# A gated recurrence with an MLP behind it: MLP products on 64 by 128 of the array in place of 64 by 64

## The chip, the core and the metric

The kernel runs on one core of one Trainium2 chip. The metric is device time in microseconds (us) of one execution. The core has five engines with queues of their own: TensorE (PE in the profile; its weight loads are listed apart as PEld), VectorE (DVE), ScalarE (ACT), GpSimd (POOL) and SyncE (SP, which here issues the DMAs). TensorE writes only to PSUM, and the other engines empty it. Each engine works through its instructions in the order in which they were issued, so that order is part of the kernel.

## The reference

An attention-like recurrence over 768 steps, for 4 batches and 8 heads of 40 channels, and behind it an MLP with a gelu. All values are float32, the MLP's weights float64 on arrival.

```python
for t in range(S):
    y[:, :, t] = einsum('bhd,bhde->bhe', rt, state)
    Sa = einsum('bhde,bhe->bhd', state, at)
    state = state * wt[:, :, None, :] - einsum('bhd,bhe->bhde', Sa, bt) \
            + einsum('bhd,bhe->bhde', vt, kt)
...
x = y.transpose(0, 2, 1, 3).reshape(B * S, H * D)      # 3072 x 320
h = x @ w_in                                           # w_in 320 x 2048
g = h * (1.0 / (1.0 + exp(-1.702 * h)))
out = g @ w_out                                        # w_out 2048 x 320
```

## The kernel before

**Units.** The sequence is cut into 12 chunks of 64 steps. A unit is one chunk of two batches with all heads; unit `i` is chunk `c = i // 2`, pair of batches `p = i % 2`, so there are 24 units. Within a chunk the recurrence is solved as matrix products: decays (`ps_cum`), scores (`ps_A`, `ps_RV`, `ps_N`), a triangular inverse in five levels (`ps_level`, then `ps_Q`, `ps_T21`), the known part (`ps_B`), the solution (`ps_X`) and the outputs with the new state (`ps_y`). From chunk to chunk goes only the state, `zraw`, so unit `i` waits for the state of unit `i - 2`, and the two units of a chunk are independent.

**The array in quarters.** Every matmul uses a quarter of TensorE's 128x128 array: 64 rows of contraction (a half of the partitions, `HALF`) by 64 columns of weights. `QUARTERS` lists the four (row half, column half) pairs, and four matmuls that follow each other go to the four quarters. One float32 matmul of the program is two MATMUL and two LDWEIGHTS instructions in the profile.

**The state's turn** (L891 to L905, in `solve`). From the second chunk on, `zr` gets the state times the decay `wz` (L891). `state_turned` then multiplies it by an identity, 16 matmuls of 64x40 weights and 40 moving columns, into `ps_zT`; two copies (L904) put it into `zT`, from which `read_state` (L907) computes `ps_rz`.

**The MLP** (`mlp`, L1021 to L1070), once for a chunk, 256 rows of x. `up(q, m, k)` is a task of 4 matmuls: quarters of 64x64 of `w_in_sb`, 256 moving columns of x. `q` counts 4 groups of the hidden width, `m` two halves of a group and `k` five steps of contraction, so a chunk has 40 up tasks. Ten of them fill one PSUM pair (two banks), and one gelu of 128x1024 (L1034) empties it to `g`. `down(p)` has 8 tasks of 8 matmuls, with 64 columns of `g` as weights and 320 moving columns of `w_out_sb`; two instructions empty `ps_down` into `ob` (L1058, L1060), and a DMA stores it.

**The order.** The kernel is first written as a list of tasks (`plan.add`), each with the engines that may take it, the time that it is thought to take there, what it reads, writes and waits for, a rank, and the PSUM pair that it holds (there are 4 pairs). `Plan.order` (L103) is a planner that runs through time: whenever an engine is free it takes the task of lowest rank that is ready. It charges TensorE for instruction fetch as well, in blocks of 256 instructions. `paced` (L223) releases MLP tasks, which have the highest ranks and so fill gaps, evenly over time; `moved` (L242) applies a table of small shifts of rank, engine and release (`FOUND`, L260). The tasks are then issued in the planned order (L1098).

**Weights.** The float64 weights come in 8 pieces and are turned into float32 by ScalarE, VectorE and GpSimd (`weight`, L466 on; `rebased` to `joined`). No up task can run before its first pieces and the first chunk's x are there.

Of the kernel before, what the change touches and what calls it, by code (L numbers as in the profile page):

```python
# [49 lines left out]
class Task:  # L50
    def __init__(self, rank, engines, fn, pair, most, size):
        self.instr, self.sbuf, self.table = engines.pop("instr", -Plan.EVENTS) + Plan.EVENTS, engines.pop("sbuf", False), engines.pop("table", None)
        self.rank, self.fn, self.pair, self.most, self.size = rank, fn, pair, most, size
        self.engines = self.may = engines
        self.after, self.then, self.release = set(), [], 0.0
        self.load = False


class Plan:

    BLOCK, FETCH, AHEAD = 256, 3460.0, 300.0
    FIRST, EVENTS = 63, 0.24
    BESIDE, LARGE, BESIDE_LARGE = 0.35, 327700, 0.5
    COLD, WINDOW, SHARE = 2.0, 2600.0, 0.45
    SWITCH = 1290.0
    DELAY = {"PE": 300.0, "DVE": 60.0, "ACT": 60.0, "POOL": 150.0, "SP": 800.0}  # L70

    BEGIN = {"PE": 0.0, "ACT": 3300.0, "DVE": 6500.0, "POOL": 10000.0, "SP": 800.0}
    LATENCY, RATE, SPREAD = 2010.0, 417.0, 1.3
# [29 lines left out]
    def order(self):  # L103
        for n, t in enumerate(self.tasks):
            t.n, t.left, t.ready, t.then = n, len(t.after), 0.0, []
        for t in self.tasks:
            for o in t.after:
                o.then.append(t)
        free = dict(self.BEGIN)
        pairs = [0.0] * self.pairs  # L110
        held, users = {}, {k: len(v) for k, v in self.of_pair.items()}
        coming = [(t.release, t.n) for t in self.tasks if not t.left]
        heapq.heapify(coming)
        able, now, wire, out, many = [], 0.0, 0.0, [], set()
        running, last, worked = [], {}, []
        table = "exp"

        def fits(t, margin=0.0):
            if t.pair is None or t.pair in held:
                return True  # L120
            clear = sum(p <= now - margin for p in pairs)
            if t.most is None:

                return clear > len({o.pair[0] for o in able if o.most is not None and o.pair not in held and not any(k[0] == o.pair[0] for k in many)})
            return clear > 0 and sum(k[0] == t.pair[0] for k in many) < t.most

        issued, begun, shared = self.FIRST, 0.0, 0.0

        def fetch(at):
            took = self.FETCH  # L130
            for _ in range(3):
                took = self.FETCH + sum(w * max(0.0, min(y, at + took) - max(x, at)) for x, y, w in running[-10:])
            return took

        def unread(t, e):

            return max((x + 60.0 for o, x in last.get(t.pair, {}).items() if o != e), default=0.0) if t.pair is not None and e != "PE" else 0.0

        def takes(t, start):

            busy = sum(max(0.0, y - max(x, start - self.WINDOW)) for x, y in worked[-60:])
            return t.engines["PE"] * (self.COLD if busy < self.SHARE * self.WINDOW else 1.0)

        def fetched(t, start):

            ns = takes(t, start) / t.instr
            at, left, block = start, t.instr, begun
            room = self.BLOCK - issued % self.BLOCK
            while left >= room:
                at += room * ns  # L150
                left -= room
                at = block = max(at, block + fetch(block))
                room = self.BLOCK
            return at + left * ns, block

        def ahead(t):

            return (issued % self.BLOCK + t.instr) * fetch(begun) / self.BLOCK - (now + takes(t, now) - begun)

        while coming or able:  # L160
            while coming and coming[0][0] <= now:
                able.append(self.tasks[heapq.heappop(coming)[1]])
            able.sort(key=lambda t: (t.rank, t.n))
            took = None
            for e in free:
                if free[e] <= now:
                    took = None
                    took = next((t for t in able if e in t.may and fits(t) and unread(t, e) <= now), None)
                    if took and e == "PE" and ahead(took) > self.AHEAD:

                        took = next((t for t in able if e in t.may and fits(t) and ahead(t) < min(self.AHEAD, ahead(took))), took)
                    if took:
                        break
            if not took:
                later = [x for x in (*free.values(), *pairs, *(unread(t, e) for t in able for e in t.may)) if now < x < float("inf")]
                later += [coming[0][0]] if coming else []
                if not later:
                    return out
                now = min(later)
                continue  # L180
            t = took
            able.remove(t)
            t.engine = e
            end = now + t.engines[e]
            if e == "ACT" and t.table:
                t.load, table = t.table != table, t.table
                end += self.SWITCH if t.load else 0.0
            if e == "PE":
                end, begun = fetched(t, now)
                worked.append((now, min(end, now + takes(t, now))))  # L190
                issued += t.instr
            if e == "POOL" or e == "DVE" and t.sbuf:

                shared = max(now, shared) + t.engines[e]
                end = max(end, shared)
            free[e] = end
            if e == "SP":
                wire = max(wire, end + self.LATENCY)
                running.append((wire, wire + self.SPREAD * t.size / self.RATE, self.BESIDE_LARGE if t.size > self.LARGE else self.BESIDE))
                end = wire = running[-1][1]  # L200
            if t.pair is not None:
                if e != "PE":
                    last.setdefault(t.pair, {})[e] = end
                if t.pair not in held:
                    held[t.pair] = next(i for i, p in enumerate(pairs) if p <= now)
                    pairs[held[t.pair]] = float("inf")
                    if t.most is not None:
                        many.add(t.pair)
                t.bank = held[t.pair]
                users[t.pair] -= 1  # L210
                if not users[t.pair]:
                    many.discard(t.pair)
                    pairs[t.bank] = end + self.DELAY[e]
            for o in t.then:
                o.ready = max(o.ready, end + (0.0 if o.engines.keys() == {e} else self.DELAY[e]))
                o.left -= 1
                if not o.left:
                    heapq.heappush(coming, (max(o.ready, o.release), o.n))
            t.start = now
            out.append(t)  # L220
        return out

    def paced(self, groups, rounds, window, share):  # L223


        best = None
        for n in range(rounds):
            out = self.order()
            end = max(t.start + t.engines[t.engine] for t in out)
            if best is None or end < best[0]:  # L230
                best = end, [(t, {**vars(t)}) for t in out]
            for g, then in zip(groups, groups[1:]):
                whole, done, begin = sum(t.engines["PE"] for t in g), 0.0, g[0].ready
                for t in g:
                    new = begin + share * (then[0].ready - begin) * done / whole - window
                    t.release = new if n == 0 else 0.5 * (t.release + new)
                    done += t.engines["PE"]
        for t, kept in best[1]:
            vars(t).update(kept)
        return [t for t, _ in best[1]]  # L240

    def moved(self, moves):  # L242

        groups = {}
        for t in self.tasks:
            key = (t.fn.__code__.co_firstlineno, t.rank, tuple(sorted(t.engines)), t.pair)
            groups.setdefault(key, []).append(t)
# [44 lines left out]
def rwkv7_gelu_quick(ctx: ExitStack, tc: tile.TileContext, time_d, v_d, w_d, wc_d, ak_d, b_d, rv_d, w_in, w_out, out):  # L292
# [60 lines left out]
    def dve(n):  # L353
        return {"DVE": 170.0 + 1.03 * n}
# [205 lines left out]
    def slot(b, u, f):  # L560
        return 4 * u + 2 * b + f
# [619 lines left out]
```

## Time and profile before

| | |
|---|---|
| time, median of 2 runs | 688.07 us (687.27 to 688.87) |
| span of the profiled execution | 685.1 us, 42187 instructions |
| mean granted TensorE clock | 0.989 of full speed |
| TensorE matmuls in the span | 19488 instructions, as many weight loads |
| of these `ps_up` / `ps_down` | 3840, busy 252.4 us / 3072, busy 240.5 us |
| gelu `g<-ps_up` 128x1024 | 48, mean 1026 ns |
| `zr<-zraw,wz` on VectorE, 128x320 | 22, median 518 ns |
| `kh<-time,G` on GpSimd, 128x320 | 19, mean 887 ns |
| chain of waits, share of the span | PE 90%, of it `ps_down` 30% and `ps_up` 29%; issue 2% |
| DMA | 69.73 MB, mean 102 GB/s |
| DMA queue of the instructions | 153 packets, 2.51 MB |

How to read it: the busy time of an engine is the time in which at least one of its instructions runs. For TensorE that is not its pace: a matmul lasts much longer than the time after which the next one may start, so four or more overlap. The pace is read from stretches in which one kind of matmul runs alone: length over count. "Issue" in the chain is time for which the profile shows no cause. A wait is charged to what ended last.

### The profile page before, as it was taken

To read this page: it belongs to the slowest core of one execution; us is meant where nothing else is said; L and a number is where in the kernel's file an instruction comes from. 1 tells how busy PE (TensorE), PEld (TensorE's weight loads), DVE (VectorE), ACT (ScalarE), POOL (GpSimd) and SP (SyncE) were. 2 spreads that over 40 slices of the span, in tenths; PEclk is the share of its full clock that TensorE was granted. 3 is DMA by queue.
4 is the path that set the end of the run, shared out by engine and by line. 5 is a ranking of instruction groups with operands and counts; after the bars stand their busy time and mean duration, and the time that the engine had idled before them with its cause. 6 is when DMAs were issued, how large, how long until landed. Compare 5 with 4: busy or idle time off the path is not lost.

```text
span 685.1 us, 42187 instructions
## 1 busy us (share of the span) xinstructions
PE 649.1 (95%) x19488; PEld 563.2 (82%) x19488; DVE 459.0 (67%) x916; ACT 323.5 (47%) x670; POOL 184.5 (27%) x215
## 2 busy tenths in 40 slices
PE   3657999999999999999999999999999999999997
PEld 3556888997899899988888897788788799899895
DVE  6686989767867767857785677867666766675001
ACT  4566633454555664564455445355354454262110
POOL 5354546324123212323213130322411421300000
PEclk9989999999999999999999999999999999999999
DMA  7993434414414413432404413413411411200100
GB/s 238 314 318 118 163 119 129 122 33 127 124 42 116 144 34 107 133 90 85 132 21 125 137 40 111 145 37 115 138 40 55 136 52 43 70 14 17 56 12 20
DMA packets 35312, 69.73 MB, mean 102 GB/s; under 512 B 5440, under 2 KB 14656, under 8 KB 35136
## 3 DMA queue, kind: packets, MB, share of 16 engines
q1 hardware_dynamic: 35136, 67.03, 32.6%
q8 instruction: 153, 2.51, 1.5%
q14 instruction: 23, 0.19, 0.1%
HBM read 59.15 MB, written 7.86 MB: 98 GB/s over the span
## 4 chain that ended last, share of the span: by engine, by line
PE 90%; DVE 3%; DMA 2%; issue 2%; ACT 1%; POOL 0%; SPq 0%; ACTq 0%; DVEq 0%
PE ps_down L343 30%; PE ps_up L343 29%; PE ps_level L343 9%; PE ps_y L343 5%; PE ps_B L343 5%; PE ps_X L343 3%; PE ps_A L343 2%; PE ps_N L343 2%; PE ps_RV L343 2%; PE ps_rz L343 1%; PE ps_zT L343 1%; PE ps_cum L343 1%; PE ps_T L343 1%; DMA rv<-in_rv 1%; DMA extra<-in_w_out 1%
## 5 line engine op out<-in xcount | busy, mean ns | idle before, releaser
L343 PE MATMUL ps_up<-xT_all,w_sb 64*64 64x256 f32 x3840 | 252.4, 377 | 1.0 <-issue 0.8
L343 PE MATMUL ps_down<-w_sb,g 64*64 64x320 f32 x3072 | 240.5, 430 | 0.5 <-issue 0.3
L343 PEld LDWEIGHTS ps_up<-xT_all,w_sb 64*64 64x64 f32 x3840 | 171.7, 133 | 15.9 <-issue 1.9
L343 PEld LDWEIGHTS ps_down<-w_sb,g 64*64 64x64 f32 x3072 | 136.1, 133 | 36.3 <-issue 1.1
L755 POOL TENSOR_TENSOR EX<-ES,quads 128x512 f32<-128x512 f32 x31 | 41.7, 1345 | 117.7 <-DVE ES L748 76.5
L1034 ACT ACTIVATE g<-ps_up 128x1024 f32<-128x1024 f32 x48 | 49.2, 1026 | 49.0 <-PE ps_up L343 48.6
L797 ACT COPY W<-ps_level 128x512 f32<-128x512 f32 x56 | 32.8, 586 | 69.3 <-PE ps_level L343 67.6
L343 PEld LDWEIGHTS ps_level<-W,EX 64*64 64x64 f32 x2560 | 59.4, 134 | 5.7 <-ACT EX L753 0.2
L799 DVE TENSOR_TENSOR E<-two,ps_level 128x256 f32<-128x256 f32 x80 | 33.1, 415 | 35.7 <-ACT W L797 32.0
L343 PE MATMUL ps_level<-W,EX 64*64 64x64 f32 (+1 forms) x2560 | 56.4, 217 | 0.0
L753 ACT ACTIVATE EX<-ES,quads 128x256 f32<-128x256 f32 x80 | 36.3, 501 | 32.5 <-DVE ES L748 31.9
L665 POOL TENSOR_TENSOR ak<-ak,FT 128x512 f32<-128x512 f32 x16 | 20.6, 1288 | 76.4 <-DMA ak<-in_ak 62.3
L343 PE MATMUL ps_level<-PT,EX 64*64 64x64 f32 (+2 forms) x1280 | 33.1, 236 | 8.3 <-DVE EX L769 4.5
L343 PEld LDWEIGHTS ps_level<-PT,EX 64*64 64x64 f32 x1280 | 30.9, 139 | 11.8 <-issue 6.5
L937 ACT COPY B<-ps_B 128x416 f32<-128x416 f32 (+1 forms) x35 | 17.2, 491 | 47.2 <-PE ps_B L343 47.0
L748 DVE STREAM_TRANSPOSE ES<-E 128x256 f32<-128x256 f32 x80 | 35.2, 442 | 4.4
L343 PE MATMUL ps_y<-M,bh 64*64 64x104 f32 (+1 forms) x768 | 35.1, 247 | 0.1
L343 PE MATMUL ps_y<-RV,kh 64*64 64x104 f32 (+1 forms) x768 | 35.1, 247 | 0.0
L999 POOL TENSOR_TENSOR x<-zr,FT 128x128 f32<-128x128 f32 x48 | 25.0, 552 | 29.7 <-DVE zr L989 14.2
L673 POOL TENSOR_TENSOR kh<-time,G 128x320 f32<-128x320 f32 x19 | 16.8, 887 | 52.4 <-PE ps_y L343 39.2
L343 PE MATMUL ps_B<-RV,A 64*64 64x104 f32 (+1 forms) x768 | 29.3, 252 | 1.4 <-issue 1.4
L343 PEld LDWEIGHTS ps_B<-RV,A 64*64 64x64 f32 x768 | 25.9, 137 | 5.4 <-issue 1.6
(136 smaller groups left out, 1111.0 us busy)
## 6 DMA issues: line engine op xcount, KB each, us to landing
time<-in_time SPq DMA_DIRECT2D x24, 320.0 KB
ak<-in_ak SPq DMA_DIRECT2D x48, 160.0 KB
rv<-in_rv SPq DMA_DIRECT2D x48, 160.0 KB
xT_all<-x_dram SPq DMA_DIRECT2D x48, 160.0 KB
wc<-in_wc SPq DMA_DIRECT2D x20, 264.0 KB
logw<-in_w SPq DMA_DIRECT2D x24, 160.0 KB
RV<-in_v SPq DMA_DIRECT2D x24, 160.0 KB
b<-in_b SPq DMA_DIRECT2D x48, 80.0 KB
```

What stands on the lines that cost most here:

```text
L343: nc.tensor.matmul(o, lhsT, rhs, start=start, stop=True, skip_group_check=True)
L665: plan.add(R, {"DVE": 690.0, "POOL": 1270.0, "sbuf": True}, lambda t: of(t.engine).tensor_mul(ahT(), ahT(), FT_of(i)), reads=T("ak", "FT") ...
L673: plan.add(R + 4, {"POOL": 870.0, "DVE": 490.0, "sbuf": True}, lambda t, n=n, dst=dst: of(t.engine).tensor_mul(dst(i)[:, :, :D], by_head(t ...
L748: plan.add(rank, dve(256), lambda t: nc.vector.transpose(ES(n), source(t)), writes=[key("ES", n, 6)], **reads)
L753: nc.scalar.activation(dst[:, :, h], ES(n), ACT.Copy, scale=quads[:, h, :1])
L755: of(t.engine).tensor_mul(dst, ES(n).unsqueeze(2).to_broadcast([128, 8, 2, 32]), quads.unsqueeze(1).to_broadcast([128, 8, 2, 32]))
L797: plan.add(rank, any2(512), lambda t: copy(t.engine)(tiles_of(W(n + 1)), blocks(psum(t, ""), 64)), writes=[key("W", n + 1, 5)], pair=pair)
L799: plan.add(rank, dve(256), lambda t: nc.vector.tensor_sub(tiles_of(E(n + 1)), every(two32, [128, 2, 4, 32]), blocks(psum(t, ""), 64)[:, :, ...
L937: plan.add(R, any2(4 * wide), lambda t: copy(t.engine)(dst(), some(psum(t, "")[:, :, :208])), writes=[("Bv", i)] if x and c > 0 else T("B" ...
L999: of(t.engine).tensor_mul(x[:, b ^ u, b], both(i)[:, at, :64], FT_of(i)[:, at])
L1034: plan.add(-45, {"ACT": 1030.0, "table": "gelu"}, lambda t: nc.scalar.activation(g_of(c * NQ + q).rearrange("p m r n -> p r m n"), psum(t, ...
```

## The change

It does five things.

1. `up` and `down` use 64 rows by 128 columns of weights instead of 64 by 64. Two matmuls, one for each half of the rows, stand where four stood; each has as many moving columns as before, and there are half as many.
2. An up task takes all five `k` (10 matmuls) and fills half of a PSUM pair's columns. So there are 8 up tasks and 8 gelus of 128x512 for each chunk, and `g` has 8 buffers of half the size.
3. The state is turned by 8 TensorE transposes of 64x128 from a new tile `zs`, which holds two heads' channels side by side, each 40 wide and padded to 64. A new product on VectorE or GpSimd fills `zs` with the same values as `zr`.
4. The planner is gone. `Plan.listed` reads the order from a text, `ORDER`, one word for each of 2388 tasks: its number, a letter for the engine (p TensorE, a ScalarE, d VectorE, g GpSimd, s SyncE) and the PSUM pair.
5. That order is another one on every engine.

```diff
+    def pe_wide(*sets):
+        return {"PE": sum(n * 2 * (cols / 1.2 + 3) for n, cols in sets), "instr": sum(8 * n for n, _ in sets), "mode": 1}
...
+            plan.add(R, {"DVE": 490.0, "POOL": 870.0, "sbuf": True}, lambda t: of(t.engine).tensor_mul(
+                zs_t[:, :, :D], zraw_of(i - 2), wz_of(i).unsqueeze(2).to_broadcast([128, 8, D])),
+                     reads=[("zraw", i - 2), ("wz", i)], room=[("zs", i)], writes=T("zs"))
...
-                    for e, f in QUARTERS:
-                        o, k = (2 * u + b) * D, slot(b, u, f) * 104 + 64
-                        mm(ps[CHANNELS[f], e, o:o + D], zr_of(i)[HALF[e], k:k + D], ident[HALF[e], :D], o == 0)
-            plan.add(R, pe((4, 40, D)), state_turned, reads=T("zr") + ([("clear", p)] if c == 1 else []), room=T("zT"), pair=("zT", i))
+                    for e in BITS:
+                        o, j = (2 * u + b) * 64, slot(b, u, 0)
+                        nc.tensor.transpose(ps[:, e, o:o + 64], zs_t[HALF[e], j:j + 2].rearrange("p f n -> p (f n)"), ident[HALF[e]])
+            plan.add(R, {"PE": 260.0, "instr": 16.0, "mode": 1}, state_turned, reads=T("zs"), room=T("zT"), pair=("zT", i))
...
-        def up(q, m, k):
+        def up(q, m):
             def go(t):
-                ph, x = psum(t, "ps_up"), xT_of(c)[:, :, k]
-                for r, h in QUARTERS:
-                    mm(ph[HALF[h], r, m * 256:(m + 1) * 256], w_in_sb[HALF[r], 2 * q + m, k, h * 64:(h + 1) * 64], x[HALF[r]],
-                       m == 0 and k == 0)
-            plan.add(R + q, pe((1, 256)), go, reads=[("xs", (c, p)) for p in BITS] + [("weight", q)],
-                     uses=[("xT", c)], room=[("g", c * NQ + q)], pair=("up", c * NQ + q), most=1)
+                ph, x = psum(t, "ps_up"), xT_of(c)
+                for k, r in product(range(NK), BITS):
+                    mm(ph[:, r, :256], w_in_sb[HALF[r], 2 * q + m, k], x[HALF[r], :, k], k == 0)
+            plan.add(R + q, pe_wide((NK, 256)), go, reads=[("xs", (c, p)) for p in BITS] + [("weight", q)],
+                     uses=[("xT", c)], room=[("g", c * NM + 2 * q + m)], pair=("up", c * NM + 2 * q + m), most=1)
...
-        def gelu(q):
-            plan.add(-45, {"ACT": 1030.0, "table": "gelu"}, lambda t: nc.scalar.activation(
-                g_of(c * NQ + q).rearrange("p m r n -> p r m n"), psum(t, "").rearrange("p r (m n) -> p r m n", m=2),
-                ACT.Gelu_apprx_sigmoid), writes=[("g", c * NQ + q)], pair=("up", c * NQ + q))
+        def gelu(n):
+            plan.add(-45, {"ACT": 640.0, "table": "gelu"}, lambda t: nc.scalar.activation(
+                g_of(n), psum(t, "")[:, :, :256], ACT.Gelu_apprx_sigmoid), writes=[("g", n)], pair=("up", n))
...
-                        for r, b in QUARTERS:
-                            o = p * 128 + b * 64
-                            mm(po[HALF[b], r, :DM], g[HALF[r], f % 2, o:o + 64], w_out_sb[HALF[r], f * DM:(f + 1) * DM], f == 0)
+                        for r in BITS:
+                            mm(po[:, r, :DM], g[HALF[r], f % 2, p * 128:(p + 1) * 128], w_out_sb[HALF[r], f * DM:(f + 1) * DM], f == 0)
...
-    plan.paced(list(paces.values()), ROUNDS, WINDOW, SHARE)
-    tasks = plan.moved(MOVES)
+    tasks = plan.listed(ORDER)
```

In `ORDER` the MLP tasks of the first chunk have the numbers 200 to 237 (up and gelu in turn, then two blocks of eight down tasks, two copies and a store); the other chunks have blocks of 38 beginning at 380, 580, 778, 976, 1174, 1372, 1570, 1768, 1966, 2162 and 2350. The turns of the state are 291, 362, 481, 562, 680, 760, 878, 958, 1076, 1156, 1274, 1354, 1472, 1552, 1670, 1750, 1868, 1948, 2066, 2144, 2258 and 2333. Three lines of it, from the beginning, where 200p3 is the first up task:

```
281a1 200p3 282a1 508s 283a1 335d2 284a1 300d0 334a2 418p1 58d 285p0 201a3 202p2 286d0 59d 511s 60d 75a 287p0 336d 61g 365p3
203a2 288d0 509s 366a3 69d 204p2 419a 301p0 67d 337p3 205a2 421g 422s 302d0 431g 338d3 208p0 433g 420a1 339d3 432d 303p2 424a
68d 317d 70g 209a0 212p1 429s 305d2 423s 304d2 306d 340p0 213a1 210p2 341a0 434g 82s 81s 83s 342d0 80s 307s 441p1 480d 211a2
```

## The prediction

> **What bounds the kernel now.** I read the page's busy times and slices first, then the busy times by stretch, then the chain of waits, then the matmul groups, and last the timeline at places where the MLP (the products `ps_up` and `ps_down`) meets the other work.
>
> ```profile
> PE 649.1 (95%) x19488; PEld 563.2 (82%) x19488; DVE 459.0 (67%) x916; ACT 323.5 (47%) x670; POOL 184.5 (27%) x215
> ...
> PE   3657999999999999999999999999999999999997
> ```
>
> TensorE is busy 95% of the span, and the slices say that what is missing lies at the start. The stretches (us, then busy us and instructions of each engine, granted clock, DMA share, GB/s) say how much:
>
> ```profile
> 0.00:25.00 25.00, 10.02 (x355) 9.17 (x359) 15.95 (x25) 10.74 (x30) 13.04 (x46) 0.99 0.84 275
> 25.00:50.00 25.00, 18.02 (x635) 16.51 (x628) 21.13 (x34) 17.11 (x39) 10.25 (x7) 0.81 0.97 307
> 50.00:75.00 25.00, 18.98 (x717) 16.88 (x720) 17.88 (x28) 14.34 (x32) 12.69 (x12) 0.93 0.49 151
> 75.00:100.00 25.00, 23.53 (x656) 20.54 (x652) 22.87 (x29) 13.94 (x36) 13.57 (x6) 1.00 0.40 136
> ...
> 300.00:450.00 150.00, 149.52 (x4550) 125.63 (x4546) 108.91 (x234) 74.79 (x144) 35.82 (x38) 1.00 0.35 100
> 450.00:600.00 150.00, 149.78 (x4656) 125.68 (x4652) 101.07 (x210) 69.63 (x148) 39.27 (x46) 1.00 0.26 77
> ```
>
> Before 100 us TensorE works 70.55 us and idles 29.45; from 300 to 600 us it idles 0.7. Busy is not yet full pace, so I checked the pace. The chain near the end (start, us, what) has MLP work alone:
>
> ```profile
> 656.49 4.32 PE ps_up L343 x80
> 660.80 1.08 PE ps_down L343 x16
> 661.88 4.32 PE ps_up L343 x80
> 666.20 14.02 PE ps_down L343 x208
> ```
>
> That is 54.0 ns per `ps_up` matmul and 67.4 per `ps_down` matmul; four run side by side, so a set of four takes 216 ns for 256 columns and 270 for 320, 0.83 ns a column and 3 ns more. At this pace the MLP is 3840 x 54.0 = 207.4 plus 3072 x 67.4 = 207.1, together 414.5 us. The timeline in mid-kernel (start, us) shows that alternation with other work costs nothing:
>
> ```profile
> 434.88 0.64 PE L343 MATMUL ps_N<-b,ak 64*64 64x64 f32 x32
> 435.35 1.26 PE L343 MATMUL ps_down<-w_sb,g 64*64 64x320 f32 x16
> 436.43 0.45 PE L343 MATMUL ps_cum<-logw,edges 64*64 64x160 f32 x8
> 436.70 2.33 PE L343 MATMUL ps_down<-w_sb,g 64*64 64x320 f32 x32
> ```
>
> `ps_N` starts 434.88 and the next piece 0.47 us later; that piece of 16 takes 1.08 to the start of its successor, exactly 16 x 67.4 ns. A change between MLP and other work is free while all share one shape: every group ends in 64*64, 64*40 or 40*64. So what adds TensorE time adds to the end, and only the 29 idle us of the start could be won elsewhere.
>
> **The change, part by part.** *Wide MLP.* Half the matmuls, each on 128 columns of weights: 1920 for `ps_up`, 1536 for `ps_down`, two side by side. The moving columns stay 256 and 320, so 960 pairs x 216 + 768 x 270 = 414.7 us: no gain, provided the wider load is hidden. The rows:
>
> ```profile
> L343 PE MATMUL ps_up<-xT_all,w_sb 64*64 64x256 f32 x3840 | 252.4, 377 | 1.0 <-issue 0.8
> ...
> L343 PEld LDWEIGHTS ps_up<-xT_all,w_sb 64*64 64x64 f32 x3840 | 171.7, 133 | 15.9 <-issue 1.9
> ```
>
> and, from the instructions that write `ps_zT` (min/median/max ns):
>
> ```profile
> L343 PEld LDWEIGHTS ps_zT<-ident,zr x704: 109/120/121, 59.7 to 603.7; 64*40 64x40 f32 x176
> ```
>
> A load of 64 columns takes 133 ns, one of 40 columns 120. So 64 columns more should add 64 x 13 / 24 = 35 ns: an estimate of 168 ns, under 216. It hides behind the matmul as the 133 do today.
>
> *Switches of shape.* The rest stays 64 by 64, so the array now changes shape between MLP and other work. In the new list I marked the entries with p (TensorE): 696, of which 288 are MLP pieces (96 up, 192 down) and 22 turns of the state, both wide; the other 386 are narrow. Along the list the shape changes 435 times; 177 wide runs are one piece long. The last 43 pieces are all wide. Before has no such change, so its price is bounded from rows. Below: 0, as the free alternation has it, and nothing speaks for a gain. Above: a matmul of `ps_up` lasts 377 ns at a pace of 216, so for 161 ns it is on its way while successors of the same shape start. If a new shape must wait for that and then for a whole load (133 to narrow, 168 to wide, mean 150), it costs 311 ns, in all 435 x 0.311 = 135 us. But after a wait the load isn't in the way in full:
>
> ```profile
> 179.50 0.40 PEld L343 LDWEIGHTS ps_up<-xT_all,w_sb 64*64 64x64 f32 x9 [0.33 <-PE ps_rz L343]
> 179.53 0.61 PE L343 MATMUL ps_up<-xT_all,w_sb 64*64 64x256 f32 x5 [0.22 <-PE ps_rz L343]
> ```
>
> The matmul starts 0.03 us behind its load, so a full emptying costs about 161 + 30 = 191 ns, 83 us in all. Some of the 161 ns is the way to the array, which may overlap. I take the middle of 0 and 191, 95 ns: 435 x 0.095 = 41.3 us. There is no cover for it, as TensorE has no idle time to lose. The Trainium skill (TensorEngine Tiling (Array Packing), Key Properties) states that changing the tiling mode drains TensorE; no run so far shows it. With the fixed part of a warm matmul of some 166 ns, which it gives in TensorE: Matmul & The Clock Gate, Single matmul latency, 435 drains would be 72 us and the sum 760, an estimate from these pages.
>
> *Longer pieces, halved gelus.* Up pieces go from 480 to 96, which saves switches (counted above) and no streaming. Gelus go from 48 of 1026 ns to 96 on 128x512; ScalarE's copies of that size take 586 (`W`) and 632 (`FT`), so 96 x 0.61 = 58.6 instead of 49.2: 9.4 us more on an engine 50% busy in mid-kernel. An up piece now waits for an emptied PSUM pair 96 times instead of 48; in the list other work mostly stands between two up pieces, longer than a gelu, so I cost this at nothing; uncovered, 9.4.
>
> *Turn of the state.* Before, 32 matmuls a unit; one such stretch begins at 305.30 and the next work at 305.67, 0.37 us, 22 times 8.1 us. After, 8 transposes. Below: one pass at the pace of 64 columns (`ps_N` above, 0.47 us for 8 sets, 58 ns a set), four pairs, 0.23 us, -3 us in all. Above: two passes paced by the 168 ns load, 1.34 us, +21. I take today's 0.37, so 0: the narrow row is the only one of the same data, and the ends widen the range. The new product `zs` goes to GpSimd 15 times (`kh`, same shape, 887 ns) and to VectorE 7 times (`zr`, 518): 13.3 and 3.6 us on engines 26% and 71% busy in mid-kernel. The turn now waits for `zs`, queued behind `zr`; behind it wait the copies of `zT` and the read of the state. TensorE meanwhile has MLP pieces, which keep it at full pace now; if that cover goes, 22 x 0.9 = 20 us at most.
>
> *New order.* The same DMAs, weight conversions and copies are issued on SP, GpSimd, VectorE and ScalarE, in another sequence. The start can gain at most its 29.45 us; a late load can cost as much. I can't tell which: 0.
>
> **The sum.** The profiled span is 685.1 us; the median of the runs is 688.07, 3 us more, which lies around the span. 688.07 + 0 (streams) + 41.3 (switches) + 0 + 0 = 729.4.
>
> **Rivals.** (1) *A better start, free switches: faster.* Place: the 29.45 idle us before 100 us. The chain has 2.0% "issue", 13.7 us, nearly all there, 12.4% of the first 100 us; the instruction queue moved 2.51 MB in 153 packets for 38,976 TensorE instructions, and the change drops 6912 of these in the MLP alone. Price: three quarters of the idle time won, 688 - 22 = 666. It leads by over 2% (13.8 us) only if a switch costs under (22 - 13.8) / 435 = 19 ns. Against it: the stalls stand where no MLP instruction is fetched yet. (2) *Switches nearly free*, up to 30 ns: 688 to 701. For it, the free alternation; against it, that row never changes shape. (3) *Full emptying and exposed loads*, 191 to 311 ns: 771 to 823. (4) *The wide load isn't hidden.* Now each quarter of the array takes a 133 ns load within each 216 ns, and streams without a gap, so loads run beside matmuls on the same rows. If that needed the narrow shape, each of 1728 pairs would wait between 30 and 168 ns for its load; at 100 ns +173 us, 902. The Trainium skill (TensorE: Matmul & The Clock Gate, What overlaps and what doesn't) says that a load overlaps running matmuls only if the row group differs; the trace disagrees in the narrow shape, and shows no wide one. That the products aren't wide is excluded by their slices in the diff.
>
> **How the numbers follow.** Forecast, a switch of 30 to 191 ns (701 to 771): 0.58. Rival 1: 0.09. Rival 2: 0.14. Rival 3: 0.11. Rival 4: 0.08. The time is the forecast's, 729. The range goes from 688 (rival 2) to 795 (inside rival 3, and the forecast with +21 for the turn); it leaves out rivals 1 and 4 and about 0.03 of rival 3. About 2% is what can be told from no change, so rival 2 is "same": faster 0.09, same 0.14, slower 0.77.
>
> **What would show it.** A pure MLP stretch at the end still at 216 and 270 ns a pair means the streams are right; more means rival 4. Between an MLP piece and other work the matmul starts should show a gap of some 95 ns more than the pace, 435 times; no gap and a span near 685 mean rival 2. Idle time before 100 us well under 29 means rival 1. The forecast is wrong if idle time after 100 us waits for gelu, `zs` or a DMA rather than lying at the changes of shape.

## The result: 757.25 us, 10.6% slower

The changed kernel takes 757.25 us (median of 2 runs, 755.02 to 759.47), against 688.07 before: 1.1057 times as long, 95% interval 1.098 to 1.1135, 69.2 us more. The profiled execution has a span of 753.3 us, 68.2 more than before.

The page, with the lines that answer to those of before:

```profile
PE 720.3 (96%) x15504; PEld 555.2 (74%) x15504; DVE 445.8 (59%) x837; ACT 366.0 (49%) x793; POOL 215.3 (29%) x265
...
PE   5578999999999999999999999999999999999997
```

TensorE has 3984 matmuls fewer and is busy 71 us longer. The stretches (us, then busy us and instructions of each engine, granted clock, DMA share, GB/s):

```profile
75.00:100.00 25.00, 24.12 (x540) 20.00 (x536) 23.51 (x29) 17.36 (x26) 16.11 (x10) 1.00 0.42 133
100.00:150.00 50.00, 48.84 (x1167) 36.94 (x1162) 39.23 (x71) 26.16 (x61) 14.72 (x17) 1.00 0.28 81
150.00:300.00 150.00, 150.00 (x3345) 115.07 (x3345) 91.18 (x180) 76.81 (x175) 43.35 (x54) 1.00 0.30 88
300.00:450.00 150.00, 148.95 (x3192) 112.31 (x3192) 95.42 (x182) 72.15 (x149) 48.88 (x56) 1.00 0.31 87
450.00:600.00 150.00, 150.00 (x3254) 113.47 (x3255) 88.41 (x175) 78.23 (x166) 41.07 (x48) 1.00 0.27 79
```

Busy time can't show the loss: TensorE is busy 448.95 of 450 us from 150 to 600 us, and the granted clock there is 1.00. The loss is in the pace, and the first question is whether the wide matmuls are slower in themselves. The chain near the end (start, us, what), where all work is wide:

```profile
714.00 4.32 PE ps_up L282 x40
718.32 1.08 PE ps_down L282 x8
719.39 2.16 PE ps_up L282 x20
721.55 1.08 PE ps_down L282 x8
```

They are not: 4.32 us for 40 is 216 ns a pair (one matmul for each half of the rows, side by side), 1.08 for 8 is 270 ns a pair, so half the instructions do the same work in the same time as before. The wide loads are hidden there, though they grew (groups of weight loads):

```profile
L282 PEld LDWEIGHTS ps_up<-xT_all,w_sb 64*128 64x128 f32 x1920 | 178.9, 187 | 27.3 <-PE ps_level L282 1.7
```

Now mid-kernel, where wide and narrow work alternate (start, us of the matmuls; the second line has the loads of the narrow piece behind the down matmuls):

```profile
405.37 1.35 PE L282 MATMUL ps_down<-w_sb,g 64*128 64x320 f32 x8
406.64 0.56 PEld L282 LDWEIGHTS ps_level<-W,EX 64*64 64x64 f32 x32 [0.44 <-issue]
406.65 0.69 PE L282 MATMUL ps_level<-W,EX 64*64 64x64 f32 x32
407.16 0.54 PE L282 MATMUL ps_B<-RV,A 64*64 64x104 f32 x16
407.52 0.54 PE L282 MATMUL ps_B<-zr,ak 64*64 64x104 f32 x16
407.99 0.54 PE L282 MATMUL ps_down<-w_sb,g 64*128 64x320 f32 x2
```

Read from start to start, the same piece of 8 down matmuls takes 1.28 us here against 1.08 at the end: 0.20 more. The narrow work behind it takes 1.34 us for 32 + 16 + 16 matmuls; at its own pace (0.46 for 32 of 64 columns, 0.36 for 16 of 104) it would take 1.18: 0.16 more. Over all matmuls after 100 us the trace gives a median of about 200 ns more than the pace (what the same matmuls take where one kind runs alone) for each wide run and 160 for each narrow one, and the medians hardly change with a run's length. Summed, the matmuls after 100 us take 75 us more than at their paces, those of the kernel before 5: 70 us more over 414 changes, 0.17 us each.

In single instructions: the next shape's first load starts 90 to 94 ns after the last matmul's columns have streamed (its start + 0.83 ns a column). Above, the last down matmul starts at 406.29 and has streamed its 320 columns at 406.55; the load starts at 406.64. The first matmul is shown to start 2 ns behind its load. But the second set follows later than usual: after a switch to the wide shape the second pair of `ps_up` starts 320 ns behind the first instead of 216, 104 more (128 columns of weights at 0.83 ns are 107); after a switch back the second set of 104 columns starts 140 ns behind the first instead of 90, 50 more (64 columns are 53). From these sizes I take it that the first matmul streams only when its load is through.

### The profile page after: what moved, and what is told of

Read it like the earlier page. It is cut to its first block, busy times and chain, and to the rows that moved or that the text cites. A ratio compares the mean times of both kernels' runs of the same rounds, so it can differ in the third digit from the quotient of the medians.

```text
span 753.3 us, 34318 instructions
## 1 busy us (share of the span) xinstructions
PE 720.3 (96%) x15504; PEld 555.2 (74%) x15504; DVE 445.8 (59%) x837; ACT 366.0 (49%) x793; POOL 215.3 (29%) x265
## 4 chain that ended last, share of the span: by engine, by line
PE 90%; DMA 5%; DVE 2%; ACT 1%; issue 0%; SPq 0%; DVEq 0%
PE ps_down L282 30%; PE ps_up L282 29%; PE ps_level L282 9%; PE ps_y L282 5%; PE ps_B L282 4%; PE ps_X L282 2%; PE ps_N L282 2%; PE ps_RV L282 2%; DMA extra<-in_w_in 2%; PE ps_rz L282 1%; PE ps_A L282 1%; DMA ak<-in_ak 1%; PE ps_T L282 1%; PE ps_Q L282 1%; PE ps_zT L849 1%; DMA w_sb<-in_w_in 1%
## 5 line engine op out<-in xcount | busy, mean ns | idle before, releaser
L282 PE MATMUL ps_down<-w_sb,g 64*128 64x320 f32 x1536 | 244.9, 447 | 0.3 <-ACT QT L807 0.3
L282 PE MATMUL ps_up<-xT_all,w_sb 64*128 64x256 f32 x1920 | 231.1, 384 | 1.6 <-DVE E L744 0.8
L282 PEld LDWEIGHTS ps_up<-xT_all,w_sb 64*128 64x128 f32 x1920 | 178.9, 187 | 27.3 <-PE ps_level L282 1.7
L282 PEld LDWEIGHTS ps_down<-w_sb,g 64*128 64x128 f32 x1536 | 137.0, 186 | 48.8 <-issue 2.9
L981 ACT ACTIVATE g<-ps_up 128x512 f32<-128x512 f32 x96 | 57.1, 595 | 130.9 <-PE ps_up L282 130.6
L698 ACT ACTIVATE EX<-ES,quads 128x256 f32<-128x256 f32 x120 | 54.2, 500 | 47.9 <-DVE ES L693 47.7
L282 PEld LDWEIGHTS ps_level<-W,EX 64*64 64x64 f32 x2560 | 45.0, 134 | 22.6 <-issue 15.8
L688 POOL TENSOR_TENSOR PT<-two,PT 128x256 f32<-128x256 f32 x20 | 14.5, 726 | 112.8 <-DVE PT L680 112.8
L742 DVE COPY W<-ps_level 128x512 f32<-128x512 f32 x30 | 20.6, 688 | 32.6 <-PE ps_level L282 32.4
L901 DVE TENSOR_TENSOR M<-ps_X,later 128x832 f32<-128x832 f32 (+1 forms) x24 | 23.9, 994 | 26.2 <-PE ps_X L282 26.1
L610 POOL TENSOR_TENSOR ak<-ak,FT 128x512 f32<-128x512 f32 x17 | 21.8, 1284 | 45.6 <-ACT FT L569 40.5
```

What stands on the lines that cost most here:

```text
L282: nc.tensor.matmul(o, lhsT, rhs, start=start, stop=True, skip_group_check=True)
L610: plan.add(R, {"DVE": 690.0, "POOL": 1270.0, "sbuf": True}, lambda t: of(t.engine).tensor_mul(ahT(), ahT(), FT_of(i)), reads=T("ak", "FT") ...
L688: plan.add(R, {"DVE": 430.0, "POOL": 750.0, "sbuf": True}, lambda t: of(t.engine).tensor_sub(at(W0_t, i)[:, :, :32], two32.unsqueeze(1).to ...
L698: nc.scalar.activation(dst[:, :, h], ES(n), ACT.Copy, scale=quads[:, h, :1])
L742: plan.add(rank, any2(512), lambda t: copy(t.engine)(tiles_of(W(n + 1)), blocks(psum(t, ""), 64)), writes=[key("W", n + 1, 5)], pair=pair)
L901: plan.add(R + 1, dve(8 * wide), lambda t: nc.vector.tensor_tensor(M_of(i)[:, :, :wide].rearrange("p (j b) n -> p b j n", b=2), some(psum( ...
```

## Experiments

Three theories stood against each other. **S**: each change of shape costs, whatever is computed. **W**: the wide matmuls cost more by themselves, 69 us over 1728 pairs. **O**: the new order, the longer pieces or the gelus cost it.

**a_all_narrow: the changed kernel without any wide shape**

```diff
-                for k, r in product(range(NK), BITS):
-                    mm(ph[:, r, :256], w_in_sb[HALF[r], 2 * q + m, k], x[HALF[r], :, k], k == 0)
+                for k in range(NK):
+                    for r, h in QUARTERS:
+                        mm(ph[HALF[h], r, :256], w_in_sb[HALF[r], 2 * q + m, k, h * 64:(h + 1) * 64], x[HALF[r], :, k], k == 0)
...
-                        for r in BITS:
-                            mm(po[:, r, :DM], g[HALF[r], f % 2, p * 128:(p + 1) * 128], w_out_sb[HALF[r], f * DM:(f + 1) * DM], f == 0)
+                        for r, b in QUARTERS:
+                            o = p * 128 + b * 64
+                            mm(po[HALF[b], r, :DM], g[HALF[r], f % 2, o:o + 64], w_out_sb[HALF[r], f * DM:(f + 1) * DM], f == 0)
...
-                    for e in BITS:
-                        o, j = (2 * u + b) * 64, slot(b, u, 0)
-                        nc.tensor.transpose(ps[:, e, o:o + 64], zs_t[HALF[e], j:j + 2].rearrange("p f n -> p (f n)"), ident[HALF[e]])
+                    for e, f in QUARTERS:
+                        o = (2 * u + b) * 64
+                        mm(ps[CHANNELS[f], e, o:o + D], zs_t[HALF[e], slot(b, u, f), :D], ident[HALF[e], :D], o == 0)
```

> The changed kernel with its order, its longer pieces, its halved gelus and zs, but the MLP and the turn of the state on quarters (64x64, the turn as matmuls by the identity): no change of shape is left of 435. Theory S (each change of shape costs about 0.17 us): 757 - 435 x 0.17 = 683, between 678 and 690. Rival O (the new order, the longer pieces or the gelus cost it): over 740. Rival W (each pair of wide matmuls costs more by itself, 69 us / 1728 = 40 ns): 688, as S.

Measured: 708.03 us against 688.02 for the kernel before on the same chip, ratio 1.0288 (1.0244 to 1.0332). O as the whole cause falls: 49 of the 69 us go with the shapes alone. But no theory had 708; S missed by 25. The order, which costs nothing visible under wide pieces, costs 20 us under narrow ones. In its trace the matmuls end 21.8 us later than before; comparing the pace in slices, 6 of these lie before 100 us (where the granted clock is 0.88 here and was 0.93) and 16 after. Waits of TensorE from 100 to 690 us (line, what for, us in total, times, longest):

```profile
PE ps_down L282 <- issue: 2.0, 3, 0.8
PE ps_Q L282 <- ACT T L698: 1.7, 1, 1.7
PE ps_rz L282 <- issue: 1.1, 1, 1.1
PE ps_level L282 <- issue: 0.9, 2, 0.8
```

In the kernel before the same view has nothing over 0.8 us in total. Some of these stalls stand in the middle of a piece, where nothing is waited for: 7.4 us after 100 us, against 1.8 before. Counted in TensorE instructions those over 0.25 us lie, in order of time, at 140, 138, 128, 100, 94, 94, 92, 82, 54, 8 and 190 modulo 256, and before at 142, 100, 58 and 24: one position in blocks of 256 that drifts slowly, which points to the instruction supply (the instruction queue moved 2.51 MB in 153 packets before and in this run, 16 KB and 255 of TensorE's 38,976 instructions each; 2.00 MB in 122 in the changed kernel, 254 of 31,008 each). About as much, 6.8 us, are gaps between pieces, of which the view names semaphore waits such as that for `T`. It looks as if the order was matched to pieces with half the instructions and 0.2 us more each. How the 20 us divide was read from the trace and not settled by a run.

**a_mlp_narrow, a_turn_narrow: one of the two goes back**

The first keeps the wide transposes and takes the first two edits above, the second takes the last edit alone.

> Only the MLP goes back to quarters; the 22 turns stay wide transposes, now each alone between narrow work, 44 changes of shape. Theory S: 44 x 0.17 = 7.5 us above a_all_narrow, about 691. Rival O: over 740. Rival W: as a_all_narrow within 2 us, since no MLP matmul is wide.

> Only the turn goes back to quarters (from zs); the MLP stays wide, 433 changes of shape instead of 435. Theory S: 757 within 4 us, as most turns stand beside a wide MLP piece. If the turn had a cost of its own worth naming, it would show here as a gain of over 5 us.

Measured: a_mlp_narrow 700.72 us, ratio 1.019 (1.015 to 1.0229), lower than a_all_narrow by 7 where 7 more was expected. It has 1056 TensorE instructions fewer, and its first 100 us lose 7 us less, at a granted clock of 0.95 against 0.88; with the order's own stalls that large, 44 changes can't be seen in the time, which tells nothing about S. The trace does show them: a turn takes 0.39 us to its successor between narrow pieces, and 0.30 in the changed kernel, where wide work mostly stands on one side. a_turn_narrow 761.15 us, ratio 1.1062 (1.1019 to 1.1105), the same as the changed kernel: the turn is not the cause, and 73.1 us over 433 changes is 0.169 us each.

**b_mlp_wide: the old order, only the shape changed**

```diff
-                for r, h in QUARTERS:
-                    mm(ph[HALF[h], r, m * 256:(m + 1) * 256], w_in_sb[HALF[r], 2 * q + m, k, h * 64:(h + 1) * 64], x[HALF[r]],
-                       m == 0 and k == 0)
+                for r in BITS:
+                    mm(ph[:, r, m * 256:(m + 1) * 256], w_in_sb[HALF[r], 2 * q + m, k], x[HALF[r]], m == 0 and k == 0)
...
-                        for r, b in QUARTERS:
-                            o = p * 128 + b * 64
-                            mm(po[HALF[b], r, :DM], g[HALF[r], f % 2, o:o + 64], w_out_sb[HALF[r], f * DM:(f + 1) * DM], f == 0)
+                        for r in BITS:
+                            mm(po[:, r, :DM], g[HALF[r], f % 2, p * 128:(p + 1) * 128], w_out_sb[HALF[r], f * DM:(f + 1) * DM], f == 0)
```

> The kernel before with its own order and pieces, only the MLP's matmuls on 64x128. Its order alternates between MLP and other work about 575 times. Theory S: 688 + 575 x 0.17 = 786, between 775 and 800, more than the changed kernel. Rival W: 688 + 69 = 757, as in the changed kernel. Rival O: about 688.

Measured: 784.84 us (2 runs), ratio 1.1408 (1.1348 to 1.1467). The trace has 579 changes of shape: 96.8 / 579 = 0.167 us each. W, which for the same number of wide pairs gave 757 us, falls; O falls too, as order, pieces and gelus are those of before. The changed kernel's longer pieces and order are thus worth 144 changes fewer.

**b_up_wide, b_down_wide: half of the MLP each**

The same edits, one at a time.

> The kernel before, its own order, only the up matmuls on 64x128. In the trace of b_mlp_wide, which has the same order, up pieces border on other shapes 364 times if the down pieces are narrow. Theory S at 0.169 us (from b_mlp_wide, 98.1 us of span over 579 changes): 688 + 61.5 = 749.5, between 744 and 755. If the cost went by the wide matmuls instead, half of b_mlp_wide's 97 us: 736.

> The same with only the down matmuls wide: 307 changes. Theory S: 688 + 51.9 = 740, between 735 and 745. By matmuls: 736. The two runs together have 671 changes against 579, so by S their extra times add up to more than that of b_mlp_wide (113 against 97 us); by matmuls they add up to the same 97.

Measured: 741.65 us, ratio 1.0841 (1.0793 to 1.0889), and 733.25, ratio 1.0709 (1.0661 to 1.0758), against 684.74 on that chip. Both are below the stated intervals. Each trace has 18 changes fewer than I had counted, 346 and 289: 56.9 / 346 = 0.164 and 48.5 / 289 = 0.168 us each. The sum, 105.4 us, is over the 96.8 of b_mlp_wide, as S has it: by 8.6 us for 56 changes more, where the miscounted 92 gave 16. The intervals leave this difference uncertain by some 6 us; S rests more firmly on the runs of work in the traces, where a wide run loses 200 ns and a narrow one 160 in these two as well.

| kernel | changes of shape | us over before | us per change |
|---|---|---|---|
| changed kernel | 435 | 69.2 | 0.159 |
| a_turn_narrow | 433 | 73.1 | 0.169 |
| b_mlp_wide | 579 | 96.8 | 0.167 |
| b_up_wide | 346 | 56.9 | 0.164 |
| b_down_wide | 289 | 48.5 | 0.168 |

The three kernels in the old order give 0.164 to 0.168 us. At that price 435 changes are 71 to 73 us, all of the changed kernel's 69.2, so nothing is left there for its order, longer pieces and gelus. The 20 us of a_all_narrow are not a share of the 69.

**a_downs_by_2, a_downs_by_4: fewer changes by grouping**

The computation is the changed kernel's. In the list each second down piece (or the last three of four) is put right behind the piece before it in its block, and the narrow work that stood between comes after:

```diff
- D0 . D1 . D2 . D3 .
+ D0 D1 . . D2 D3 . .          (by 2)
+ D0 D1 D2 D3 . . . .          (by 4)
```

> The changed kernel, with all its wide matmuls, but in the list each second down piece of a block stands right behind the first (from the second chunk on): 337 changes of shape instead of 435. Theory S at 0.17 us: 757 - 98 x 0.17 = 740, between 736 and 747. Rival W (wide pairs cost more by themselves): 757. Rival O, in the form that the order of the changed kernel makes TensorE wait: no lower than 752, since the waits stay.

> The same in groups of four down pieces: 281 changes of shape. Theory S: 757 - 154 x 0.17 = 731, between 727 and 742; narrow work now waits up to 4.3 us for a group, so some of it can come back as idle time of TensorE. Rival W: 757.

Measured: 769.65 us, ratio 1.1176 (1.1094 to 1.1258), and 809.22, ratio 1.1747 (1.1672 to 1.1821): slower than the changed kernel, where S promised 740 and 731; by the times alone, O's "no lower than 752" for the first would stand. The changes did go, and their price in the traces is the same (the medians of a wide and a narrow run are still about 200 and 160 ns), but another cost came. The stretches of a_downs_by_4:

```profile
300.00:450.00 150.00, 134.58 (x2788) 104.58 (x2786) 81.37 (x160) 66.23 (x143) 47.06 (x53) 0.94 0.29 81
450.00:600.00 150.00, 134.25 (x2801) 104.96 (x2801) 80.23 (x161) 67.21 (x136) 30.70 (x35) 0.98 0.26 69
```

TensorE now idles 31 us in these 300, against 1 in the changed kernel. The granted clock falls as well, to 0.94 and 0.98: for 27 us after 100 us it was half, and a group of 32 down matmuls at 309.21 took 7.00 us where others take 4.51. That can be up to 14 of the 52 us over the changed kernel; in a_downs_by_2 the clock stayed at 1.00 there. The timeline of a_downs_by_4 shows how the idle time comes about, between two groups of down pieces:

```profile
316.42 0.46 PE L282 MATMUL ps_cum<-logw,edges 64*64 64x160 f32 x8
317.21 0.94 PE L282 MATMUL ps_X<-B,T 64*64 64x104 f32 x32 [0.33 <-DVE T L821]
317.98 0.54 PE L282 MATMUL ps_B<-RV,A 64*64 64x104 f32 x16
318.33 0.54 PE L282 MATMUL ps_B<-zr,ak 64*64 64x104 f32 x16
319.50 0.59 PE L282 MATMUL ps_B<-RV,A 64*64 64x104 f32 x16 [0.62 <-ACT B L885]
```

Two of the narrow steps wait, `ps_X` for VectorE and the second `ps_B` for ScalarE, which work on the step before. In the changed kernel these lines stand between the same steps, the first between `ps_cum` and `ps_X`, the second between the two pairs of `ps_B` pieces (start, us):

```profile
303.04 2.42 PE L282 MATMUL ps_down<-w_sb,g 64*128 64x320 f32 x16
306.98 1.35 PE L282 MATMUL ps_down<-w_sb,g 64*128 64x320 f32 x8
```

There neither step waits. With the pieces in one group, the steps stand bare. So the switches were the price of cover, and in this order the cover was worth more than the switch.

**b_cols32, b_rows128: what counts as another shape**

```diff
-                    mm(ps[HALF[b], u, e * 64:e * 64 + 64], at(Tc_t, i)[HALF[u], 32 * j:32 * j + 64], QT[HALF[u], b, e], e == 0)
+                    for s in (0, 32):
+                        mm(ps[64 * b + s:64 * b + s + 32, u, e * 64:e * 64 + 64], at(Tc_t, i)[HALF[u], 32 * j + s:32 * j + s + 32], QT[HALF[u], b, e], e == 0)
```

```diff
-                    mm(ps[HALF[u], b, :160], incl[HALF[b]], lw[HALF[b], n * 160:(n + 1) * 160], True)
+                    mm(ps[HALF[u], b, :160], incl, lw[:, n * 160:(n + 1) * 160], True)
```

> The kernel before, but in off_two each matmul of 64x64 is two of 64x32 (the same values; 32 more instructions a unit): 24 tasks, 48 changes if 32 columns count as another shape. If any change of the column tile costs what 64 to 128 columns costs: 48 x 0.17 = 8 us more, 696, and gaps of some 0.1 us ahead of and behind ps_T21. If only the wide shape is special: 688 within 2 us, no gaps.

> The kernel before, but the matmuls of ps_cum contract all 128 rows at once (128x64; the sums of decays then add both halves, so the output is another): 24 tasks, 48 changes of the row tile. If a change of rows costs as much as one of columns: 696, with gaps at ps_cum; and as two such matmuls no longer run beside the other rows', ps_cum itself takes longer, 8 matmul instructions two by two at 135 ns, 0.54 us instead of 0.27, 24 times 6.5 us: 702 in all. If a change of rows is free: 694.

Measured: b_cols32 698.84 us against 688.88, ratio 1.0136 (1.0073 to 1.0199); b_rows128 699.36, ratio 1.015 (1.0085 to 1.0214): 10.0 and 10.5 us more, where the theories of a price gave 8 and 14 and a free change 0 and 6. The total alone would leave b_rows128 open; the traces decide. The timeline of b_cols32, then of b_rows128:

```profile
270.36 0.46 PE L343 MATMUL ps_T<-QT,Tc 64*32 64x64 f32 x32
270.74 1.31 PE L343 MATMUL ps_down<-w_sb,g 64*64 64x320 f32 x16
```

```profile
484.64 0.76 PE L343 MATMUL ps_cum<-logw,edges 128*64 128x160 f32 x8
485.34 0.69 PE L343 MATMUL ps_RV<-rv 64*64 64x64 f32 x32
```

`ps_T` takes 0.38 us to its successor, where 16 matmuls of 64x64 take 0.23. `ps_cum` takes 0.70, where four pairs at the traced 136 ns are 0.54. In both traces the next shape's load starts 90 to 95 ns after the last columns have streamed, into the odd shape and out of it, as in the changed kernel. So it is not the wide shape alone that costs: each of the three changes of the tile's rows or columns tried here does. A matmul of 64x40 or 40x64 among those of 64x64, which the kernel before has, is no such change: there it kept full pace.

No experiment beat the kernel before, and none pointed to a version that would: its TensorE has no shape to change and little pace to win after 100 us (some 5 us).

## Why the prediction came out as it did

The direction and the mechanism were right: 729 us forecast, 757 measured, inside 688 to 795.

- *Wide streams cost nothing*: right. The pairs run at 216 and 270 ns. The wide load measured 187 ns against the estimate of 168, and stays under the pace.
- *435 changes of shape*: the count was exact. **The term that was mis-sized** is their price, "I take the middle of 0 and 191, 95 ns". End to end a change costs 0.16 to 0.17 us, close to the upper end, so the term was about 69 us rather than 41.3. Two readings led there. The low end of 0 came from a row in which the shape doesn't change, and so said nothing about a change. And the upper end was built of the wrong parts: 161 ns for a matmul's tail and 30 for the load, because the matmul is shown to start 0.03 us behind its load. In the trace the emptying is 90 ns and the load delays the work by 104 or 50 ns; a matmul's start in the profile is not the start of its streaming. That 161 + 30 = 191 comes near the measured sum is luck.
- The drain that the Trainium skill states (TensorEngine Tiling (Array Packing), Key Properties) fits what the trace shows, 90 ns without streaming or a load at each change; the figure of 760 us from its 166 ns lies near 757, but by luck, as the parts differ.
- *Longer pieces, halved gelus*: right at nothing. 96 gelus of 595 ns are busy 57.1 us against 49.2, and no wait of a matmul is put down to one (of loads, 1.1 us in all).
- *Turn of the state*: right at 0. Next to wide work a turn takes 0.30 us to its successor, as the typical one of before does (0.30, not the 0.37 that I read at one place), and a_turn_narrow is no faster. `zs` cost nothing.
- *New order, 0*: right for this kernel (the first 100 us idle 26.0 us instead of 29.45), but for a reason that I hadn't given. The order has some 20 us of stalls of its own, seen when the shapes go; presumably the slower TensorE pieces covered them.
- *Rivals*: a better start with free switches and nearly free switches are excluded by the 200 and 160 ns. Exposed loads at 191 to 311 ns a change were too dear, as the emptying is 90 and not 161. A wide load that isn't hidden is excluded by the pace at the end. The rule of the Trainium skill behind that rival (TensorE: Matmul & The Clock Gate, What overlaps and what doesn't), that a load overlaps running matmuls only with another row group, disagrees with this trace in the wide shape too: each half of the rows takes a load of 187 ns within each 216 ns of streaming.

## What to carry to other kernels

Where TensorE sets the time, count the places in program order at which the tile's rows or columns change, and charge each the 0.17 us of these float32 pieces; a shape that halves the instructions but differs from its neighbours can lose far more than it saves. Don't group work to save such changes before asking what the pieces between dependent steps were hiding. And an order found for one kernel is not neutral in another: here it cost 20 us as soon as all pieces were narrow.

## What the hardware showed that I had not expected

- The price of a change is the same in kind for 64 to 128 columns, 64 to 32 columns and 64 to 128 rows: 90 to 95 ns from the end of streaming to the next load, and then a delay that for 64 and 128 columns of weights (50 and 104 ns) goes with the columns loaded.
- The TensorE transpose of float32 loads its 128 columns in less time than a matmul of the same width: 139 ns a load against 187, and its pairs start 62 ns apart.
- Wide pieces relieve the instruction supply, 122 packets instead of 153, but as TensorE in the kernel before lost only 1.8 us to mid-piece stalls after 100 us, there was nothing to win.
